# Pairs of pooled attention on Trainium2: values multiplied ahead of later scores, and chunks 3 to 5 made known twelve steps sooner

## The chip, the cores and the metric

The kernel runs on one core of one Trainium2 chip. The metric is device time of one execution in microseconds; a lower one is better. The other cores of the chip are idle.

## The reference

An attention is followed by two feed-forward networks, all in fp32:

```
q, k, v: 4 batches, 8 heads, 576 positions, 64 wide
pooled:  q, k, v averaged over groups of 4 positions (144 of them), softmax(q k^T / 8) v, each row repeated 4 times
local:   softmax of q k^T / 8 where |i - j| < 4, times v
x = pooled + local, as 2304 rows of 512
h = x @ w_in (512 x 2048);   x2 = (h * cos h) @ w_out (2048 x 512)
out = (((x2 @ w1) * (x2 @ w2)) @ w3) @ w_out2    (w1, w2: 512 x 1024, w3: 1024 x 1024)
```

## The kernel before, in words

The program is one long order of instructions, which a small planner in the kernel writes at build time: it holds a list of jobs (Python generators), each with an urgency (a lower number goes first), and a guess of how long every operation takes (`cost`, `LATENCY`). Whenever an engine is free in that guess, it is given the first job in the order of urgency whose inputs are ready by the guess. On the chip each engine then follows its own list in order, with semaphores between the engines. All operations go through one helper, so that nearly every instruction carries its line, L137 (L138 in the changed kernel); groups are told apart by their tiles.

The stages, in the order in which TensorE (PE) comes to them:

- **Weights w3 and w_out2** are multiplied into one matrix (`w5_job`, tile `ps_w`), with the attention of the first chunks between them. PE fills what is left with products of zeros (`ps_z`, `ps_w<-zeros`).
- **First network.** The rows are cut into 6 chunks of 384. A step is a chunk and one of the 16 slices of the inner width, 96 steps in all: `h_job` makes `ps_h` (12 products), `chain_job` turns it into g = h cos h on ScalarE (ACT), VectorE (DVE) and GpSimd (POOL), and `y_job` adds g times w_out to four banks (12 products, `ps_y`). The h of a step may be up to four steps ahead of its y (`LAG`). Chunk 0 takes 12 of its steps (`HALF`), then chunk 1 comes in.
- **Second network** (`ps_ab`, `ps_o`), from step 96 on.

The attention runs beside it. Its local part is done in units of 192 positions, two to a chunk (`unit_job`; scores `ps_sb`, softmax in `sc`, transposes `ps_tb`, values `ps_av`, then the sum with the pooled part in `xs`). Its pooled part is done in pairs of heads, four to a batch (`pair_job`; scores `ps_s`, softmax in `sd`, transposes `ps_t`, copies `ptp` of these, products with values `ps_t<-ptp` or `ps_p<-ptp`, result `up`). A unit needs all four pairs of its batch before its values, and h of a chunk needs both of its units. Batches 0 and 1 take the softmax of a pair's scores straight from PSUM with a bias; batches 2 and 3 through `sd` and GpSimd.

In `pair_job` the products of pair p - 1 with its values go right behind the transposes of pair p, in columns 288 to 431 of the first of the two banks that these fill, and ACT then reads `up` from there. Four PSUM banks (`bank`) are shared by h and the attention; while h runs, the attention may hold two of them (`banks`). A pair's `ptp` and `vd` have one buffer each, `sd` two. ACT holds one table of functions at a time, and exp of the attention and sin of the chain are in different ones, so each visit of exp during the first network costs two table loads; `exps` gathers waiting ones.

The loop at the end of `fused_kernel` tells the planner of a chunk's attention when h has reached a step: of chunk 2 early, and of chunk i from 3 on when the first step of chunk i - 1 is done (`first[i - 1] + 1`, which is 33, 49 and 65).

Of the kernel before, what the change touches and what calls it, by code (L numbers as in the profile page):

```python
# [14 lines left out]
AF = mybir.ActivationFunctionType  # L15
# [5 lines left out]
B, H, S, D = 4, 8, 576, 64  # L21
# [7 lines left out]
KC = DM // P  # L29
SD = S // 4  # L30
# [16 lines left out]
HALF = 12  # L47
# [8 lines left out]
EARLY_WARM, RISEN, REST = 3000.0, 10000.0, 130.0  # L56
FIRST, SLACK = 3000.0, 1150.0
TOGETHER, PATIENCE = 4, 6750.0
A0, A1 = 6.0, 6

U_QK, U_PAIR, U_POOL, U_UNIT = -12, -14, -10.5, -9.0
# [14 lines left out]
def fused_kernel(ctx: ExitStack, tc: tile.TileContext, qk_block, v_block, qk_pool, v_pool,  # L76
# [96 lines left out]
    def buf(slot, name, shape, dtype=F32):  # L173

        pool, size, _ = slots[slot[0]]
        item = 8 if dtype == I64 else 4
        t = pool.tile([P, size // item], dtype, name=name, tag=f"{slot[0]}{slot[1]}", bufs=1)
        t = t[:, :math.prod(shape)]
        if len(shape) == 1:
            return t  # L180
        names = "abcd"[:len(shape)]
        return t.rearrange(f"p ({' '.join(names)}) -> p {' '.join(names)}", **dict(zip(names, shape)))
# [6 lines left out]
    def bank(n, name):  # L189

        return psum.tile([P, 512], F32, name=name, tag=f"bank{n}", bufs=1)
# [18 lines left out]
    def on(name, fn, *aps, when=lambda: True):  # L210
        yield name, fn, aps, when

    def until(cond):
        while not cond():
            yield "until", cond
# [4 lines left out]
    def take(name, n=1, spare=lambda: 0):  # L220

        yield from until(lambda: len(at_hand(name)) >= n + spare())
        got = at_hand(name)[:n]
        for x in got:
            free[name].remove(x)
        return got[0][1] if n == 1 else [x[1] for x in got]
# [15 lines left out]
    def give(name, slot, engine):  # L242
        free[name].append((ends[engine] + LATENCY[engine], slot))
# [5 lines left out]
    def count(key, n=1):  # L249
        done[key] = done.get(key, 0) + n  # L250

    def reached(key, n):
        return lambda: done.get(key, 0) >= n


    def banks(n):
        yield from until(lambda: done.get("banks", 0) + n <= (2 if done.get("h", 0) else 4))
        count("banks", n)
        got = []
        for _ in range(n):  # L260
            got.append((yield from take("bank")))
        return got
# [146 lines left out]
    up_t = {}  # L409
# [42 lines left out]
    with_values = {}  # L452

    def pair_job(b, p):
        early, bias = b < EARLY, b < BIAS
        yield from until(reached("sd", b * KC + p))
        fs = yield from take("sd")
        count("sd")
        f = buf(fs, "sd", [2, 2, SD])[:QP]
        sums, nms = small(fs, "sums", [2, 2], QP), small(fs, "nm", [2, 2], QP)  # L460
        if early:
            yield from until(reached(("pooled", b), UPB))
            qk = pool_qk[b][0][:, p]
        else:
            qs = yield from take("qkd")
            raw_slot = yield from take("raw")
            raw = buf(raw_slot, "qkr", [2, SD, 4])
            yield from on("sy", lambda: sy.dma_start(out=raw, in_=qk_pool[b, p]))
            qk = buf(qs, "qkd", [2, SD])
            for side in range(2):  # L470
                yield from on("ve", lambda: ve.tensor_reduce(out=qk[:, side], in_=raw[:, side], axis=AX.X, op=ALU.add), raw)
            give("raw", raw_slot, "ve")
        ns = yield from banks(2)
        ps = [bank(n, "ps_s") for n in ns]

        def scores():

            for c in range(2):
                for r in range(2):
                    rs = slice(r * D, (r + 1) * D)  # L480
                    pe.matmul(ps[r][:QP, c * SD:(c + 1) * SD], lhsT=qk[rs, 0, c * QP:(c + 1) * QP], rhs=qk[rs, 1, :], start=True, stop=True)

        yield from on("pe", scores, qk)
        if not early:
            give("qkd", qs, "pe")
        elif p == KC - 1:
            give("raw", pool_qk[b][1], "pe")
        for r in range(2):
            s, nm = ps[r][:QP, :2 * SD].rearrange("p (c k) -> p c k", c=2), nms[:, r]
            yield from on("ve", lambda: ve.tensor_reduce(out=nm, in_=s, axis=AX.X, op=ALU.max, negate=True), ps[r])  # L490
            if bias:
                continue
            yield from on("ve", lambda: ve.tensor_tensor(out=f[:, r], in0=s, in1=nm.unsqueeze(2).to_broadcast([QP, 2, SD]), op=ALU.add), nms)
            give_bank(ns[r], "ve")
        if bias:
            yield from on("ve", lambda: ve.tensor_scalar_mul(nms, nms, SCALE / 16.0), nms)

            def exp():
                for r in range(2):
                    for c in range(2):  # L500
                        se.activation(out=f[:, r, c], in_=ps[r][:QP, c * SD:(c + 1) * SD], func=AF.Exp, scale=SCALE / 16.0,
                                      bias=nms[:, r, c:c + 1], accum_out=sums[:, r, c:c + 1])
                    give_bank(ns[r], "se")

            yield from exps(exp, nms)
        else:
            yield from exps(lambda: se.activation(out=f, in_=f, func=AF.Exp, scale=SCALE / 16.0), f)
            yield from on("ve", lambda: ve.tensor_reduce(out=sums, in_=f, axis=AX.X, op=ALU.add), f)

        def div():  # L510
            ve.tensor_scalar_add(sums, sums, 1e-9)
            ve.reciprocal(sums, sums)

        yield from on("ve", div, sums)
        each, by = ("ve", ve) if b < BY_VE else ("ge", ge)
        yield from on(each, lambda: by.tensor_tensor(out=f, in0=f, in1=sums.unsqueeze(3).to_broadcast([QP, 2, 2, SD]), op=ALU.mult), sums)

        yield from until(lambda: not p or (b, p - 1) in with_values)
        before = with_values.pop((b, p - 1)) if p else None
        ns = yield from banks(2)  # L520
        psts = [bank(n, "ps_t") for n in ns]

        def turn():
            for r in range(2):
                for kc in range(2):
                    for c in range(2):
                        o = (kc * 2 + c) * QP
                        pe.transpose(psts[r][:QP, o:o + QP], f[:, r, c, kc * QP:(kc + 1) * QP], ident[:QP, :QP])

        def values(of, pso):  # L530
            v, t = of[:2]
            for kc in range(2):
                for r in range(2):
                    pe.matmul(pso[r * D:(r + 1) * D], lhsT=v[:, kc, r * D:(r + 1) * D], rhs=t[:, r, kc * SD:(kc + 1) * SD], start=kc == 0, stop=kc == 1)
            give("vd", of[2], "pe")
            give("ptp", of[3], "pe")

        if b not in up_t:
            slot = yield from take("up")
            up_t[b] = buf(slot, "up", [KC, SD]), slot  # L540
        up = up_t[b][0]
        if p:
            pso = psts[0][:, 2 * SD:3 * SD]
            yield from on("pe", lambda: (turn(), values(before, pso)), f, *before[:2])
        else:
            yield from on("pe", turn, f)
        give("sd", fs, "pe")
        tsl = yield from take("ptp")
        t = buf(tsl, "ptp", [2, 2 * SD])[:QP]
        for r in (1, 0):  # L550
            yield from on("se", lambda: se.copy(t[:, r], psts[r][:QP, :2 * SD]), psts[r])
            if r == 0 and p:
                yield from on("se", lambda: se.activation(out=up[:, p - 1, :], in_=pso, func=AF.Copy, scale=0.25), psts[0])
                count(("pairs", b))
            give_bank(ns[r], "se")
        yield from until(lambda: (b, p) in pool_vs)
        v, vs = pool_vs.pop((b, p))
        if p < KC - 1:
            with_values[b, p] = v, t, vs, tsl
            return  # L560
        n = (yield from banks(1))[0]
        pso = bank(n, "ps_p")
        yield from on("pe", lambda: values((v, t, vs, tsl), pso[:, :SD]), v, t)
        yield from on("se", lambda: se.activation(out=up[:, p, :], in_=pso[:, :SD], func=AF.Copy, scale=0.25), pso)
        give_bank(n, "se")
        count(("pairs", b))
# [484 lines left out]
    with tc.manual_schedule():  # L1051
# [60 lines left out]
        Job(W5 + 1000.5, y_job())  # L1112
        attention(1, W5 + first[1] - A1)
        for i in range(2, NC1):
            run(reached("h", first[i - 1] + 1 if i > 2 else first[0] + HALF + 1))
            attention(i, W5 + first[i])
            if i == 2:
                for f in range(F2):
                    Job(W5 + first[2] + 4 * f, w12_job(f))
# [68 lines left out]
```

## Time and profile before

| | |
|---|---|
| median of 3 runs | 845.57 us (843.66 to 848.01) |
| span of the profiled execution, first to last instruction (the profile has no other time of it) | 843.8 us |
| PE busy | 827.2 us (98%) |
| DVE, ACT, POOL busy | 515.3, 444.1, 371.5 us |
| mean granted clock of TensorE | 0.996 |
| chain of waits, share of PE | 87% |

Times in the rows are counted from the first instruction. A busy PE is one with a matrix product under way; "idle before" is the time in which an engine had nothing under way, and the arrow names what ended it. The granted clock is 1.00 at 2.4 GHz and 0.50 at 1.2 GHz. A matrix product in fp32 (scores, values, transposes, `ps_w`) shows as two records.

### The profile page before, as it was taken

To read this page: it belongs to the slowest core of one execution; us is meant where nothing else is said; L and a number is where in the kernel's file an instruction comes from. 1 tells how busy PE (TensorE), PEld (TensorE's weight loads), DVE (VectorE), ACT (ScalarE), POOL (GpSimd) and SP (SyncE) were. 2 spreads that over 40 slices of the span, in tenths; PEclk is the share of its full clock that TensorE was granted. 3 is DMA by queue.
4 is the path that set the end of the run, shared out by engine and by line. 5 is a ranking of instruction groups with operands and counts; after the bars stand their busy time and mean duration, and the time that the engine had idled before them with its cause. 6 is when DMAs were issued, how large, how long until landed. Compare 5 with 4: busy or idle time off the path is not lost.

```text
span 843.8 us, 15678 instructions
## 1 busy us (share of the span) xinstructions
PE 827.2 (98%) x5982; PEld 752.2 (89%) x5982; DVE 515.3 (61%) x924; ACT 444.1 (53%) x900; POOL 371.5 (44%) x330
## 2 busy tenths in 40 slices
PE   7999999999999999999989999999999999999998
PEld 7544599999999999999989999999999899999997
DVE  5987889995547785778566434734435544463442
ACT  2746698877767676867658565632113211231112
POOL 0112559865443355434635434524335632363322
PEclk9999999999999999999999999999999999999999
DMA  9998896131445553545452328692001400020002
GB/s 268 289 309 288 290 343 240 41 113 50 150 143 169 151 161 118 169 144 158 139 165 73 101 100 301 246 402 99 26 13 53 149 26 26 24 90 26 26 26 75
DMA packets 61402, 121.87 MB, mean 144 GB/s; under 512 B 18960, under 2 KB 26384, under 8 KB 61328
## 3 DMA queue, kind: packets, MB, share of 16 engines
q1 hardware_dynamic: 54432, 112.12, 41.4%
q10 hardware_dynamic: 6896, 8.76, 3.0%
q8 instruction: 47, 0.77, 0.4%
q14 instruction: 27, 0.22, 0.1%
HBM read 93.07 MB, written 27.79 MB: 143 GB/s over the span
## 4 chain that ended last, share of the span: by engine, by line
PE 87%; DVE 5%; ACT 3%; DMA 2%; issue 1%; POOL 1%; ACTq 0%; SPq 0%; DVEq 0%; POOLq 0%
PE ps_y L137 21%; PE ps_ab L137 20%; PE ps_h L137 20%; PE ps_o L137 12%; PE ps_w L137 7%; DVE t L137 3%; PE ps_t L137 2%; PE ps_av L137 1%; PE ps_tb L137 1%; PE ps_s L137 1%; PE ps_sb L137 1%; DVE c L137 1%; DMA vr<-v_pool 1%; POOL wo L137 1%; ACT c L137 1%
## 5 line engine op out<-in xcount | busy, mean ns | idle before, releaser
L137 PE MATMUL ps_h<-xs,wi 128*128 128x384 f32 x1152 | 221.7, 339 | 3.3 <-DVE c L137 2.2
L137 PE MATMUL ps_y<-g,wo 128*128 128x384 f32 x1152 | 220.9, 337 | 0.5 <-POOL g L137 0.5
L137 PEld LDWEIGHTS ps_h<-xs,wi 128*128 128x128 f32 x1152 | 201.3, 189 | 7.2 <-DVE c L137 2.5
L137 PEld LDWEIGHTS ps_y<-g,wo 128*128 128x128 f32 x1152 | 199.8, 188 | 2.9 <-issue 1.5
L137 PE MATMUL ps_ab<-y,w 128*128 128x384 f32 x1008 | 184.9, 336 | 0.9 <-DVE v L137 0.8
L137 PEld LDWEIGHTS ps_ab<-y,w 128*128 128x128 f32 x1008 | 176.7, 188 | 6.6 <-issue 1.4
L137 DVE TENSOR_TENSOR v<-v,ps_ab 128x384 f32<-128x384 f32 x168 | 90.8, 553 | 134.9 <-ACT w L137 74.0
L137 POOL TENSOR_TENSOR g<-c,g 128x384 fp32r<-128x384 f32 x96 | 107.3, 1118 | 145.4 <-ACT g L137 125.8
L137 ACT ACTIVATE c<-c 128x384 f32<-128x384 f32 x192 | 100.5, 524 | 34.4 <-DVE c L137 31.6
L137 POOL TENSOR_TENSOR v<-v 128x384 f32<-128x384 f32 x48 | 49.7, 1038 | 145.2 <-DVE v L137 143.4
L137 PE MATMUL ps_o<-w,m 128*128 128x512 f32 x432 | 107.3, 392 | 0.0
L137 ACT CAST m<-v 128x384 fp32r<-128x384 f32 x48 | 24.5, 514 | 142.9 <-POOL v L137 142.9
L137 PEld LDWEIGHTS ps_o<-w,m 128*128 128x128 f32 x432 | 80.3, 188 | 14.1
L137 DVE SCALAR_TENSOR_TENSOR c<-turns,ps_h 128x384 f32<-128x384 int32 x96 | 52.7, 549 | 63.0 <-ACT turns L137 61.1
L137 DVE SCALAR_TENSOR_TENSOR c<-c,ps_h 128x384 f32<-128x384 f32 x96 | 52.7, 549 | 46.5 <-ACT c L137 46.2
L137 ACT CAST g<-c 128x384 fp32r<-128x384 f32 x96 | 49.2, 512 | 37.1 <-DVE c L137 35.0
L137 ACT ACTIVATE turns<-ps_h 128x384 int32<-128x384 f32 x96 | 46.8, 487 | 36.7 <-PE ps_h L137 36.0
L137 PE MATMUL ps_w<-w,w 128*128 128x512 f32 x128 | 59.5, 604 | 1.0 <-DVE w L137 1.0
L137 ACT ACTIVATE t<-raw 128x512 f32<-128x512 f32 x72 | 47.8, 677 | 15.9 <-DMA raw<-w3t 3.4
L137 DVE TENSOR_SCALAR t<-t 128x512 int32<-128x512 int32 x72 | 51.0, 723 | 7.6 <-ACT t L137 7.6
L137 POOL TENSOR_TENSOR m<-v,m 128x384 fp32r<-128x384 f32 x48 | 47.8, 1016 | 0.0
L137 POOL TENSOR_TENSOR sc<-sc,bmax 128x1024 f32<-128x1024 f32 x12 | 24.3, 2026 | 49.4 <-DVE bmax L137 39.7
(89 smaller groups left out, 856.7 us busy)
## 6 DMA issues: line engine op xcount, KB each, us to landing
w_sc<-w SPq DMA_DIRECT2D x56, 256.0 KB
w<-w_sc SPq DMA_DIRECT2D x28, 512.0 KB
raw<-w SPq DMA_DIRECT2D x24, 512.0 KB
raw<-w3t SPq DMA_DIRECT2D x16, 512.0 KB
raw<-w_in SPq DMA_DIRECT2D x16, 512.0 KB
raw<-w_out SPq DMA_DIRECT2D x16, 512.0 KB
qkr<-qk_pool SPq DMA_DIRECT2D x12, 576.0 KB
vb<-v_block SPq DMA_DIRECT2D x48, 128.0 KB
```

The lines of the kernel that those rows point to most:

```text
L137: return call(*args, **kw)
```

## The change

In `pair_job` the products of a pair with its values move: those of pair p - 2 now go in front of the scores of pair p (p = 2, 3), in the same columns of the first scores' bank, in one piece with these scores, and ACT reads `up` from there ahead of DVE's maxima. Only pair 2's products still go behind pair 3's transposes, and pair 3's own come last, as before. So pair p's scores now ask that pair p - 2's copies are made, and the transposes of pairs 1 and 2 ask that the scores of the pair behind are done. And the planner hears of the attention of chunks 3, 4 and 5 when h has reached 21, 37 and 53 instead of 33, 49 and 65. Numbers of instructions stay the same, but for one product of zeros less on PE (11 in `ps_w` instead of 12) and two more table loads on ACT (24 instead of 22).

```
--- before.py
+++ after.py
@@ -56,6 +56,7 @@
 EARLY_WARM, RISEN, REST = 3000.0, 10000.0, 130.0
 FIRST, SLACK = 3000.0, 1150.0
 TOGETHER, PATIENCE = 4, 6750.0
+AHEAD = 12
 A0, A1 = 6.0, 6
 
 U_QK, U_PAIR, U_POOL, U_UNIT = -12, -14, -10.5, -9.0
@@ -470,8 +471,22 @@
             for side in range(2):
                 yield from on("ve", lambda: ve.tensor_reduce(out=qk[:, side], in_=raw[:, side], axis=AX.X, op=ALU.add), raw)
             give("raw", raw_slot, "ve")
+        yield from until(lambda: p < 2 or (b, p - 2) in with_values)
+        before = with_values.pop((b, p - 2)) if p >= 2 else None
         ns = yield from banks(2)
         ps = [bank(n, "ps_s") for n in ns]
+        if b not in up_t:
+            slot = yield from take("up")
+            up_t[b] = buf(slot, "up", [KC, SD]), slot
+        up = up_t[b][0]
+
+        def values(of, pso):
+            v, t = of[:2]
+            for kc in range(2):
+                for r in range(2):
+                    pe.matmul(pso[r * D:(r + 1) * D], lhsT=v[:, kc, r * D:(r + 1) * D], rhs=t[:, r, kc * SD:(kc + 1) * SD], start=kc == 0, stop=kc == 1)
+            give("vd", of[2], "pe")
+            give("ptp", of[3], "pe")
 
         def scores():
 
@@ -480,7 +495,14 @@
                     rs = slice(r * D, (r + 1) * D)
                     pe.matmul(ps[r][:QP, c * SD:(c + 1) * SD], lhsT=qk[rs, 0, c * QP:(c + 1) * QP], rhs=qk[rs, 1, :], start=True, stop=True)
 
-        yield from on("pe", scores, qk)
+        if before:
+            pso = ps[0][:, 2 * SD:3 * SD]
+            yield from on("pe", lambda: (values(before, pso), scores()), qk, *before[:2])
+            yield from on("se", lambda: se.activation(out=up[:, p - 2, :], in_=pso, func=AF.Copy, scale=0.25), ps[0])
+            count(("pairs", b))
+        else:
+            yield from on("pe", scores, qk)
+        count(("scores", b))
         if not early:
             give("qkd", qs, "pe")
         elif p == KC - 1:
@@ -515,8 +537,9 @@
         each, by = ("ve", ve) if b < BY_VE else ("ge", ge)
         yield from on(each, lambda: by.tensor_tensor(out=f, in0=f, in1=sums.unsqueeze(3).to_broadcast([QP, 2, 2, SD]), op=ALU.mult), sums)
 
-        yield from until(lambda: not p or (b, p - 1) in with_values)
-        before = with_values.pop((b, p - 1)) if p else None
+        last = p == KC - 1
+        yield from until((lambda: (b, p - 1) in with_values) if last else reached(("scores", b), p + 2) if p else lambda: True)
+        before = with_values.pop((b, p - 1)) if last else None
         ns = yield from banks(2)
         psts = [bank(n, "ps_t") for n in ns]
 
@@ -527,19 +550,7 @@
                         o = (kc * 2 + c) * QP
                         pe.transpose(psts[r][:QP, o:o + QP], f[:, r, c, kc * QP:(kc + 1) * QP], ident[:QP, :QP])
 
-        def values(of, pso):
-            v, t = of[:2]
-            for kc in range(2):
-                for r in range(2):
-                    pe.matmul(pso[r * D:(r + 1) * D], lhsT=v[:, kc, r * D:(r + 1) * D], rhs=t[:, r, kc * SD:(kc + 1) * SD], start=kc == 0, stop=kc == 1)
-            give("vd", of[2], "pe")
-            give("ptp", of[3], "pe")
-
-        if b not in up_t:
-            slot = yield from take("up")
-            up_t[b] = buf(slot, "up", [KC, SD]), slot
-        up = up_t[b][0]
-        if p:
+        if last:
             pso = psts[0][:, 2 * SD:3 * SD]
             yield from on("pe", lambda: (turn(), values(before, pso)), f, *before[:2])
         else:
@@ -549,13 +560,13 @@
         t = buf(tsl, "ptp", [2, 2 * SD])[:QP]
         for r in (1, 0):
             yield from on("se", lambda: se.copy(t[:, r], psts[r][:QP, :2 * SD]), psts[r])
-            if r == 0 and p:
+            if r == 0 and last:
                 yield from on("se", lambda: se.activation(out=up[:, p - 1, :], in_=pso, func=AF.Copy, scale=0.25), psts[0])
                 count(("pairs", b))
             give_bank(ns[r], "se")
         yield from until(lambda: (b, p) in pool_vs)
         v, vs = pool_vs.pop((b, p))
-        if p < KC - 1:
+        if not last:
             with_values[b, p] = v, t, vs, tsl
             return
         n = (yield from banks(1))[0]
@@ -1112,7 +1123,7 @@
         Job(W5 + 1000.5, y_job())
         attention(1, W5 + first[1] - A1)
         for i in range(2, NC1):
-            run(reached("h", first[i - 1] + 1 if i > 2 else first[0] + HALF + 1))
+            run(reached("h", first[i - 1] + 1 - AHEAD if i > 2 else first[0] + HALF + 1))
             attention(i, W5 + first[i])
             if i == 2:
                 for f in range(F2):
```

The planner answers with another order on every engine. Three places matter for the prediction.

**PE, the first steps of the first network** (`ps_sb` and `ps_tb` are of local units, `ps_s` and `ps_t` of batch 1's pairs). Before:

```order
L137 MATMUL ps_sb<-kb,qb 64x64 x32
L137 MATMUL ps_w_919<-w_750,w_973 128x512
L137 MATMUL ps_h<-xs,wi 128x384 x48
L137 MATMUL ps_t<-ident,sd 72x72 x8
L137 MATMUL ps_t<-ptp,vd 64x144 x4
L137 MATMUL ps_y_1403<-g,wo 128x384 x3
L137 MATMUL ps_y_1434<-g,wo 128x384 x3
```

And in the changed kernel:

```order
L138 MATMUL ps_sb<-kb,qb 64x64 x32
L138 MATMUL ps_w_895<-w_777,w_996 128x512
L138 MATMUL ps_w_903<-w_777,w_996 128x512
L138 MATMUL ps_w_923<-w_777,w_996 128x512
L138 MATMUL ps_h<-xs,wi 128x384 x48
L138 MATMUL ps_y_1374<-g,wo 128x384 x3
L138 MATMUL ps_s<-ptp,vd 64x144 x4
L138 MATMUL ps_s<-qkd 72x144 x4
L138 MATMUL ps_y_1389<-g,wo 128x384 x3
```

The transposes and values that stood between the first four steps of h and the first y are gone from there; the pair's next piece (values and scores) comes only behind the first three products of y.

**POOL, around its first g** (`wi`, `wo`: weights of the first network; `sc`: a unit's softmax; `g`: the low half of a step's g). Before:

```order
L137 TENSOR_TENSOR xs<-xb,xs 128x2x4x48
L137 TENSOR_TENSOR wo<-t,wo 128x512
L137 TENSOR_TENSOR g<-c,g 128x384 x3
L137 TENSOR_TENSOR sc<-sc,bmax 128x1024
L137 TENSOR_TENSOR wi<-t,wi 128x512
```

In the changed kernel:

```order
L138 TENSOR_TENSOR xs<-xb,xs 128x2x4x48 x2
L138 TENSOR_TENSOR wo<-t,wo 128x512
L138 TENSOR_TENSOR sc<-sc,bmax 128x1024
L138 TENSOR_TENSOR g<-c,g 128x384
L138 TENSOR_TENSOR wi<-t,wi 128x512
L138 TENSOR_TENSOR g<-c,g 128x384
```

The unit's `sc` has moved from behind the third g to in front of the first.

**PE, h step 64, the first of chunk 4.** Before, from the values of chunk 4's second unit on (`ps_y` has four banks, each with its number):

```order
L137 MATMUL ps_y_4296<-g,wo 128x384 x3
L137 MATMUL ps_av<-pt,vb 64x48 x32
L137 MATMUL ps_y_4303<-g,wo 128x384 x3
...
L137 MATMUL ps_y_4296<-g,wo 128x384 x3
L137 MATMUL ps_y_4303<-g,wo 128x384 x3
L137 MATMUL ps_h<-xs,wi 128x384 x33
L137 MATMUL ps_sb<-kb,qb 64x64 x32
```

The nine rows of y behind these values are 27 products. In the changed kernel, at the same step (the `ps_av` here is of chunk 5's first unit; chunk 4's two stand in front of h steps 49 and 57):

```order
L138 MATMUL ps_h<-xs,wi 128x384 x12
L138 MATMUL ps_y_4561<-g,wo 128x384 x3
L138 MATMUL ps_av<-pt,vb 64x48 x32
L138 MATMUL ps_y_4589<-g,wo 128x384 x3
L138 MATMUL ps_y_4597<-g,wo 128x384 x3
L138 MATMUL ps_y_4602<-g,wo 128x384 x3
L138 MATMUL ps_h<-xs,wi 128x384 x12
```

Where h ran out of x and y was used up before, a step of h and a step of y now alternate without a break.

## Rows read from the trace of the kernel before

**Rows 1.** The page: span, busy time of each engine, PE's granted clock in 40 slices.

```profile
span 843.8 us, 15678 instructions
PE 827.2 (98%) x5982; PEld 752.2 (89%) x5982; DVE 515.3 (61%) x924; ACT 444.1 (53%) x900; POOL 371.5 (44%) x330
PEclk9999999999999999999999999999999999999999
```

**Rows 2.** Waits of PE: who waited for whom, us in total, times, longest.

```profile
PE ps_h L137 <- DVE c L137: 2.2, 1, 2.2
...
PE ps_sb L137 <- DVE sc L137: 1.3, 1, 1.3
PE ps_s L137 <- DVE sc L137: 1.2, 1, 1.2
...
PE ps_h L137 <- POOL wi L137: 1.1, 2, 0.8
...
PE ps_tb L137 <- POOL sc L137: 0.4, 1, 0.4
```

**Rows 3.** Timeline of PE around h step 64: start, us, operation, records, idle before.

```profile
413.23 4.95 PE L137 MATMUL ps_y<-g,wo 128*128 128x384 f32 x27
418.03 4.33 PE L137 MATMUL ps_h<-xs,wi 128*128 128x384 f32 x24
424.55 3.25 PE L137 MATMUL ps_h<-xs,wi 128*128 128x384 f32 x9 [2.20 <-DVE c L137]
...
435.11 1.16 PE L137 MATMUL ps_sb<-kb,qb 64*64 64x64 f32 x64 [0.25 <-issue]
```

**Rows 4.** Windows there: length, busy by engine (records), granted clock, DMA, GB/s.

```profile
422.00:424.00 2.00, 0.35 (x2) 0.03 (x1) 0.06 (x1) 1.57 (x4) 0.00 (x0) 1.00 0.96 356
424.00:426.00 2.00, 1.45 (x5) 1.45 (x6) 0.96 (x2) 1.73 (x4) 0.88 (x1) 0.61 0.03 12
426.00:428.00 2.00, 2.00 (x18) 1.56 (x21) 0.56 (x1) 0.58 (x2) 0.84 (x2) 0.53 0.00 0
428.00:430.00 2.00, 2.00 (x70) 1.93 (x63) 1.01 (x2) 0.31 (x1) 0.28 (x1) 1.00 0.04 8
```

**Rows 5.** Timeline of PE, first steps of the first network.

```profile
102.87 8.89 PE L137 MATMUL ps_h<-xs,wi 128*128 128x384 f32 x48
111.61 0.41 PE L137 MATMUL ps_t<-ident,sd 72*72 72x72 f32 x4
112.24 0.44 PE L137 MATMUL ps_t<-ident,sd 72*72 72x72 f32 x4 [0.22 <-DVE c L137]
112.61 0.71 PE L137 MATMUL ps_t<-ptp,vd 72*64 72x144 f32 x8
113.78 2.35 PE L137 MATMUL ps_y<-g,wo 128*128 128x384 f32 x12 [0.46 <-POOL g L137]
```

**Rows 6.** Timeline of POOL in the same stretch.

```profile
110.42 1.90 POOL L137 TENSOR_TENSOR wo<-t,wo 128x512 fp32r<-128x512 f32 x1 [4.72 <-ACT wo L137]
112.27 2.42 POOL L137 TENSOR_TENSOR g<-c,g 128x384 fp32r<-128x384 f32 x2
...
120.70 1.90 POOL L137 TENSOR_TENSOR sc<-sc,bmax 128x1024 f32<-128x1024 f32 x1 [0.80 <-DMA raw<-w_in]
```

**Rows 7.** Timeline of ACT in the same stretch.

```profile
107.22 1.28 ACT L137 ACT_TABLE_LOAD   x1
108.52 0.53 ACT L137 ACTIVATE c<-c 128x384 f32<-128x384 f32 x1
...
117.35 1.07 ACT L137 ACTIVATE sc<-sc 128x1024 f32<-128x1024 f32 x1
```

**Rows 8.** Timeline of DVE in the same stretch.

```profile
109.95 0.54 DVE L137 SCALAR_TENSOR_TENSOR c<-c,ps_h 128x384 f32<-128x384 f32 x1
...
118.45 1.22 DVE L137 TENSOR_REDUCE bmax<-sc 128x16 f32<-128x1024 f32 x1 [0.16 <-ACT sc L137]
```

**Rows 9.** Timeline of PE at the longest wait of steps 12 to 20.

```profile
171.62 1.62 PE L137 MATMUL ps_sb<-kb,qb 64*64 64x64 f32 x64 [1.32 <-DVE sc L137]
```

**Rows 10.** Window behind that wait, columns as in rows 4.

```profile
172.00:174.00 2.00, 1.92 (x67) 1.85 (x68) 2.00 (x5) 1.66 (x4) 2.00 (x2) 1.00 0.27 98
```

**Rows 11.** Groups of ACT: busy us, mean ns, idle before.

```profile
L137 ACT ACTIVATE up<-ps_t 128x144 f32<-128x144 f32 x12 | 3.6, 299 | 0.0
```

## Prediction

> **What bounds the kernel now.** I read the page first: of the 843.8 us of the span PE has a product under way in 827.2, and its clock is granted in full in nearly every slice [rows 1]. The products stay the same, so the change can win only what PE loses: the 16.6 us in which it is idle, and any stretch at half clock. The waits of PE then say where these lie [rows 2]. The longest one is 2.2 us, before h, released by a c on DVE; waits of 1.3, 1.1 (two of them) and 0.4 us lie in the first twenty steps. The others stand ahead of the first network or in the second one, where the change alters little.
>
> The timeline shows what the longest wait is [rows 3]. Nine rows of y run in one piece, 27 products: h of step 64 lacks its x, because chunk 4's attention is late, and y eats up the four steps that h was ahead. Then h makes two steps, nothing is left for y, and PE stands for 2.20 us, until the chain of ACT, DVE and POOL has freed a bank. The windows show a second price [rows 4]: from 424 to 428 the granted clock is 0.61 and 0.53, so the 1.2 GHz level after that idle time, and 1.00 again from 428. At 171.62 PE was idle for 1.32 us [rows 9] and the clock stayed at 1.00 [rows 10].
>
> The second stretch to read is the start of the first network [rows 5]. Four steps of h run from 102.87 to 111.61; the first y starts at 113.78. Of these 2.17 us only 0.22 + 0.46 = 0.68 are idle: a pair's transposes and values fill the other 1.49.
>
> **A, the stall at step 64.** In the new order the units of chunk 4 are done eight and more steps ahead, and h and y alternate there. The 2.20 us go, the 0.25 of the scores behind it [rows 3], and the half clock: (1 - 0.61) x 2 + (1 - 0.53) x 2 = 1.72 us [rows 4]. A = -4.2. The ends are -4.2 and 0 (another chunk starves instead). The attention's own products only change their place.
>
> **B, the first y.** The filler of 1.49 us is gone from its gap; its work comes later and takes its time there. With g as early as before, PE idles the whole 2.17 instead of 0.68. Is g as early? Before, the first g on POOL starts at 112.27, behind a wo of 1.90 [rows 6]. Now the unit's sc, also 1.90, stands between that wo and g; and this sc needs an exp of 1.07 on ACT, which now runs ahead of the table load [rows 7], and a sum of 1.22 on DVE, which now runs ahead of the first c that leaves the chain at 109.95 [rows 8]. Before, both came after it (117.35 and 118.45). The wo is done earlier in exchange. So g comes between 0 and 1.9 us later; I take 0.5, since one GpSimd piece of 1.90 stands directly ahead of g in either order. That is a gap of 2.7 with nothing in it, 2.0 more than the 0.68. Such a gap is longer than the 2.20 that was followed by the low clock and twice the 1.32 that was not, so I add 1.72. B = +3.7. Its ends are 0 (the gap closes by another order of arrival) and 2.17 + 1.90 - 0.68 + 1.72 = +5.1.
>
> The Trainium skill, "TensorE: Matmul & The Clock Gate", Part 1, says that the gate has just these two levels, and that the same kernel shows a different number of slow products from one run to the next. By that the 1.72 of A and of B may each be absent from a run; A + B would lie between -2.2 (slow stretch in A alone) and +1.2 (in B alone), against -0.5 in my sum. The rows agree on the two levels; one profile cannot show the scatter.
>
> **C, the other waits of steps 1 to 20.** The two waits for wi (1.1 us together [rows 2]) come from a POOL that works without a break; its sc of 1.90 at 120.70 [rows 6] is now done before them. I let them go: C = -1.1. The waits of 1.32 and 0.4 I leave as they are. Ends: all 2.8 go, or as much comes on top.
>
> **What I cost at nothing.** Two more table loads, 1.28 each [rows 7]: ACT is busy for 53% [rows 1], and h is up to four steps ahead of y. Where that lead is used up, a visit of exp is on the path, with its loads. One product of zeros less: under 0.2. The moved products ahead of the first network: PE is full there, and what is done later frees as much time now; a new wait in this in-order list could cost 0 to 1.2, as its nearest row (`ps_s` for DVE [rows 2]). The DMAs: the last load of a pair's q and k of batch 1 and the loads of chunks 3 to 5 move on SP; those of 3 to 5 come sooner, and no wait of PE names a load. The weights of the second network are ready about two steps later, still ahead of step 96.
>
> A wait is added: ACT's read of `up` and DVE's maxima of the scores now share a bank, so the maxima follow a read of 0.30 us [rows 11] eight times, and the chain's pieces on DVE stand behind them. The lead of h hides it; in the open it would be 2.4 us at least. The Trainium skill, "PSUM — Partial Sum Buffer", on bank collisions, says that two engines may not use one bank and quadrant at once, reads included; that is why this is a wait and not an overlap. No row here shows its price.
>
> **Sum.** -4.2 + 3.7 - 1.1 = -1.6 us: a span of 842.2. The span of before lies 1.8 below the median of the runs, 845.57, so the time is 845.57 - 1.6 = **844.0 us**. A measurement of this kernel can tell about 0.5% from no change, 4.2 us; the forecast is no change.
>
> **Rivals.**
>
> *The gap at the first y does not open* (faster): the chain comes sooner, or the order of arrival puts the pair's scores into it. For it: h starts some 2 us sooner, while DVE and ACT have their conversions of weights behind them earlier. Against it: the banks for these scores are freed only by the c of the chain. Then -4.2 - 1.1 = -5.3: 840.3 us. With the gap as it is but no slow clock, -3.3: 842.3, still no change.
>
> *The early attention takes the lead of h away* (slower). One mechanism: visits of exp put loads of 2 x 1.28 and the exp of 1.07 between a step's two pieces on ACT, now spread over chunks 2 to 4, with the new wait on DVE in the same steps. It decides when a chain is late by more than the lead of h, some three steps of about 4.2 us (a step of h and one of y). Each such place costs what step 64 cost, 2.20 + 1.72 = 3.9. With two of them: -1.6 + 7.8 = +6.2, 851.8 us. Against it: before, ten such visits passed without a wait of PE.
>
> *The stall only moves* (no change): x of chunk 2, whose second unit now ends two steps ahead of its use, is late in place of chunk 4. Then A = 0, and the sum is +2.6: 848.2.
>
> **How the numbers follow.** Forecast 0.45, gap closed 0.30, lead lost 0.15, stall moved 0.10. The forecast case reaches below -4.2 in a few parts of a hundred, when more of C goes. So faster by over 0.5% 0.32, within 0.5% 0.53, slower 0.15. The range takes in A, and all of C with B at 0, -7.0, at the low end (838.5), and at the high end the moved stall with a late g (850); it leaves out the rival of lost lead.
>
> **What would show it.** Right: no run of more than about 12 products of y without h at step 64, and a clock of 1.00 there; PE idle for 2 to 3.5 us between the first four steps of h and the first y, released by g of POOL, with a clock near 0.5 for some 3.5 us behind it; waits for wi under 0.5. Wrong: a full PE at the first y (then the first rival), or new waits of h or y for a c or a g between steps 20 and 66 (then the second), or at step 32 (then the third).

## The result, and the profile after

The changed kernel takes 852.35 us (median of 6 runs, 850.61 to 855.41) against 846.22 for the kernel before (6 runs beside it): 6.1 us more, a ratio of 1.0080 with a 95% interval of 1.0063 to 1.0097. It is slower, by more than the 0.5% that can be told from no change, and lies above the range of the prediction (838.5 to 850).

The page of the changed kernel (span, busy time, granted clock in 40 slices), for [rows 1]:

```profile
span 853.5 us, 15677 instructions
PE 832.0 (97%) x5981; PEld 754.6 (88%) x5981; DVE 521.9 (61%) x924; ACT 446.7 (52%) x902; POOL 374.5 (44%) x330
...
PEclk9899979999999999999999999999999999999999
```

PE is idle for 21.5 us instead of 16.6, and two slices show a lower clock. The one in the second lies ahead of the first network, and it does not come from the order of instructions: e9 below has the same order and a 9 there. This profile is of the longest of the six runs (mean clock 0.988, the others 0.992 to 0.994), and the runs of the kernel before alone have mean clocks of 0.993 to 1.000. The 7 in the sixth slice is the place to read. The view of waits, for [rows 2]:

```profile
PE ps_y L138 <- POOL g L138: 5.1, 1, 5.1
...
PE ps_h L138 <- DVE c L138: 1.2, 1, 1.2
```

The 2.2 us of h for a c, step 64, are gone. In their place stands one wait of 5.1 us: the first y. The timeline of PE there, for [rows 5]:

```profile
104.91 8.89 PE L138 MATMUL ps_h<-xs,wi 128*128 128x384 f32 x48
118.93 1.33 PE L138 MATMUL ps_y<-g,wo 128*128 128x384 f32 x3 [5.12 <-POOL g L138]
120.18 1.23 PE L138 MATMUL ps_s<-ptp,vd 72*64 72x144 f32 x8
121.34 1.24 PE L138 MATMUL ps_s<-qkd 64*72 64x144 f32 x8
122.51 4.21 PE L138 MATMUL ps_y<-g,wo 128*128 128x384 f32 x12
126.52 2.42 PE L138 MATMUL ps_h<-xs,wi 128*128 128x384 f32 x12
```

From the first h to the fifth step of h it took 21.61 us. In the kernel before it was 13.10, from 102.87 [rows 5] to the start of the fifth step:

```profile
115.97 2.24 PE L137 MATMUL ps_h<-xs,wi 128*128 128x384 f32 x12
```

That stretch of before has three products of y less, which are 0.52 at the 2.08 us that twelve take from start to start. So the stretch lost 8.0 us. Windows, columns as in [rows 4]:

```profile
116.00:118.00 2.00, 0.00 (x0) 0.00 (x0) 2.00 (x4) 2.00 (x6) 1.95 (x2) 0.65 0.79 184
...
124.00:126.00 2.00, 2.00 (x8) 2.00 (x7) 2.00 (x5) 1.97 (x5) 1.72 (x2) 0.50 1.03 412
126.00:128.00 2.00, 2.00 (x11) 2.00 (x10) 2.00 (x4) 0.75 (x2) 0.72 (x1) 0.79 1.03 414
420.00:430.00 10.00, 10.00 (x116) 9.70 (x115) 5.42 (x10) 7.73 (x13) 4.17 (x4) 1.00 0.37 120
```

The clock falls while PE stands and stays at its lower level until 126 to 128; around step 64 (last row) it is 1.00 and PE is never idle. There h and y alternate, for [rows 3]:

```profile
426.33 0.69 PE L138 MATMUL ps_y<-g,wo 128*128 128x384 f32 x3
426.94 1.15 PE L138 MATMUL ps_av<-pt,vb 64*64 64x48 f32 x64
428.02 1.83 PE L138 MATMUL ps_y<-g,wo 128*128 128x384 f32 x9
429.69 2.24 PE L138 MATMUL ps_h<-xs,wi 128*128 128x384 f32 x12
```

Why g is late, ACT tells (timeline, for [rows 7]; `DMA_DIRECT2D` is a store of `w5_out_job`, the profile writes its tile without the number):

```profile
104.41 0.33 ACTq L132 DMA_DIRECT2D w_sc<-w  x1
...
107.59 0.49 ACT L138 ACTIVATE turns<-ps_h 128x384 int32<-128x384 f32 x1
111.84 0.66 ACT L138 ACTIVATE t<-raw 128x512 f32<-128x512 f32 x1 [3.75 <-DMA w_sc<-w]
112.40 1.05 ACT L138 ACTIVATE sc<-sc 128x1024 f32<-128x1024 f32 x1
113.46 1.28 ACT L138 ACT_TABLE_LOAD   x1
114.76 0.52 ACT L138 ACTIVATE c<-c 128x384 f32<-128x384 f32 x1
...
116.94 0.50 ACT L138 CAST g<-c 128x384 fp32r<-128x384 f32 x1
```

A conversion of a weight (`t<-raw`) stands ahead of the unit's exp and of the first sin. It waits 3.75 us for a store. In the kernel before a conversion stands in the same place, ahead of the table load, and it waits for nothing:

```profile
106.55 0.66 ACT L137 ACTIVATE t<-raw 128x512 f32<-128x512 f32 x1
```

POOL of the changed kernel, for [rows 6]:

```profile
107.66 1.36 POOL L138 TENSOR_TENSOR wo<-t,wo 128x512 fp32r<-128x512 f32 x1 [1.77 <-ACT wo L138]
115.57 1.90 POOL L138 TENSOR_TENSOR sc<-sc,bmax 128x1024 f32<-128x1024 f32 x1 [6.55 <-DVE bmax L138]
117.52 1.35 POOL L138 TENSOR_TENSOR g<-c,g 128x384 fp32r<-128x384 f32 x1
```

POOL is done with wo early and stands for 6.55 us until exp and sum have come through. g starts 12.61 us behind h's start; before it was 9.40.

### The profile page after: what moved, and what is told of

It is laid out like the page before. It is cut to its first block, busy times and chain, and to the rows that moved or that the text cites. A ratio compares the mean times of both kernels' runs of the same rounds, so it can differ in the third digit from the quotient of the medians.

```text
span 853.5 us, 15677 instructions
## 1 busy us (share of the span) xinstructions
PE 832.0 (97%) x5981; PEld 754.6 (88%) x5981; DVE 521.9 (61%) x924; ACT 446.7 (52%) x902; POOL 374.5 (44%) x330
## 4 chain that ended last, share of the span: by engine, by line
PE 83%; DVE 8%; DMA 4%; issue 2%; ACT 2%; POOL 1%; SPq 0%; ACTq 0%; DVEq 0%; POOLq 0%
PE ps_ab L138 20%; PE ps_y L138 20%; PE ps_h L138 19%; PE ps_o L138 12%; PE ps_w L138 7%; DVE t L138 4%; PE ps_s L138 2%; PE ps_av L138 1%; DVE c L138 1%; PE ps_t L138 1%; PE ps_sb L138 1%; DVE bmax L138 1%; DMA w_sc<-w 1%; PE ps_tb L138 1%; DMA vr<-v_pool 1%
## 5 line engine op out<-in xcount | busy, mean ns | idle before, releaser
L138 PE MATMUL ps_y<-g,wo 128*128 128x384 f32 x1152 | 223.9, 340 | 5.1 <-POOL g L138 5.1
L138 PE MATMUL ps_w<-w,w 128*128 128x512 f32 x128 | 62.4, 630 | 1.0 <-DVE w L138 1.0
L138 DVE TENSOR_SCALAR t<-t 128x512 int32<-128x512 int32 x72 | 55.4, 783 | 8.9 <-ACT t L138 8.6
L138 PEld LDWEIGHTS ps_w<-w,w 128*128 128x128 f32 x128 | 23.9, 198 | 26.4 <-issue 23.0
```

The source lines that it names most:

```text
L138: return call(*args, **kw)
```

## The experiments

All are compared with the kernel before, run beside them on the same chip. The stretch is that from the first h to the fifth step of h, less 0.52 for three more products of y where they lie in it; its loss is against 13.10. In e8 the idle time does not stand at the first y but ahead of it, around the fourth step of h.

| run | median us | ratio, 95% | idle at first y | loss of stretch |
|---|---|---|---|---|
| the change | 852.35 | 1.0063 to 1.0097 | 5.12 | 8.0 |
| e1, no notice | 878.07 | 1.0365 to 1.0408 | 5.33 | 7.6 |
| e2, notice only | 845.49 | 0.9979 to 1.0007 | 0.47 | 0.0 |
| e3, late pairs | 841.95 | 0.9945 to 0.9968 | 0.47 | 0.0 |
| e4, g slots | 847.96 | 1.0019 to 1.0045 | 5.93 | 8.8 |
| e5, no store wait | 845.05 | 0.9980 to 1.0000 | 0.89 | 1.0 |
| e6, filled gap | 848.83 | 1.0019 to 1.0046 | filled | 5.5, with 5.4 of filler |
| e7, batch 1 as before | 843.80 | 0.9961 to 0.9987 | 1.59 | 2.1 |
| e8, batch 0 as before | 848.12 | 1.0007 to 1.0034 | 2.34 + 2.09 | 6.3 |
| e9, same order | 848.81 | 1.0028 to 1.0055 | 3.25 | 5.6 |
| e10, late pairs, no notice | 856.98 | 1.0111 to 1.0155 | 0.47 | 0.0 |
| e11, notice of 16 | 845.01 | 0.9982 to 1.0009 | 0.47 | 0.0 |

### The parts of the change

By the notice is meant the number of steps by which the planner hears of a chunk's attention sooner (`AHEAD`). e1 is the changed kernel with `AHEAD = 0`, e2 the kernel before with `- AHEAD` in the loop, e3 the change with

```
-        yield from until(lambda: p < 2 or (b, p - 2) in with_values)
-        before = with_values.pop((b, p - 2)) if p >= 2 else None
+        moved = b >= 2
+        yield from until(lambda: not moved or p < 2 or (b, p - 2) in with_values)
+        before = with_values.pop((b, p - 2)) if moved and p >= 2 else None
...
+        behind = last or not moved and p > 0
```

and `behind` in place of `last` where the transposes are made. The first 20 steps are ordered as in the changed kernel in e1, and as in the kernel before in e2 and e3.

> The changed kernel with the planner told of chunks 3 to 5 as late as before; the first 20 steps are in the changed kernel's order, and the plan lets y use up h's whole lead at two steps, 48 and 64. Theory (the loss lies at the first y, the gain at step 64): the loss stays and the gain goes, with a second stall at step 48: +4 to +8 against the changed kernel, 856 to 860 us, 10 to 14 above before; PE idle over 3 us at the first y and over 1.5 us at step 64. Rival (the early notice takes the lead of h away and makes the loss): below the changed kernel, 845 to 849, with no idle time over 1 us between steps 20 and 66 that the changed kernel lacks.

> The kernel before with the earlier notice alone; its order is that of before up to some step 29. Theory: the gain of step 64 without the loss at the first y: 4 us less than before, 841 to 843; no idle time over 1 us at step 64, 0.7 us at the first y. Rival (early notice is what costs): 848 to 852, with new waits of h or y between steps 20 and 66.

> The whole change, but the values move only in batches 2 and 3; the order is that of before up to some step 29. Theory: as the notice alone, 841 to 843, within 1.5 us of it, since the moved values of later batches have h's lead above them. Rival (the moved values cost in every batch, by the new wait of DVE on ACT): 4 or more above the notice alone, 846 to 850.

e1 is 25.7 us above the change where I expected 4 to 8, and not in the way of the rival: the idle time of the first y stayed, and two long stalls came, at steps 48 and 64. Waits of its timeline around step 64:

```profile
445.39 1.97 PE L138 MATMUL ps_tb<-ident,sc 128*128 128x128 f32 x8 [9.27 <-POOL sc L138]
452.54 7.20 PE L138 MATMUL ps_h<-xs,wi 128*128 128x384 f32 x24 [3.29 <-POOL xs L138]
```

e2 lost nothing at the first y and has no stall at step 64 (clock 1.00 and PE full from 400 to 430), as the theory had it; but its time is that of before, not 4 us less. e3 is what the theory gave, 4.2 us below before by the medians (0.43% by the ratio, interval 0.32 to 0.55%), and the fastest of all kernels here. Its windows around step 64:

```profile
416.00:426.00 10.00, 10.00 (x118) 9.66 (x119) 4.61 (x12) 6.96 (x16) 6.72 (x8) 1.00 0.52 161
426.00:436.00 10.00, 10.00 (x59) 10.00 (x58) 5.90 (x10) 7.30 (x16) 2.33 (x3) 1.00 0.46 158
```

So the loss lies with the values moved in the early batches, 0 and 1; with the earlier notice the stall at step 64 is gone, in e2 as in e3. Why e2 stays behind e3 I did not settle. Two new waits are part of it, from its timeline:

```profile
243.22 0.63 PE L138 MATMUL ps_tb<-ident,sc 128*128 128x128 f32 x4 [0.87 <-DVE sums L138]
...
316.94 0.82 PE L138 MATMUL ps_t<-ident,sd 72*72 72x72 f32 x8 [0.39 <-DVE sc L138]
```

e3 has only 0.24 us of such waits from step 20 to step 72. The same kind of scatter showed in two more runs of e3's code, with `AHEAD` at 0 (e10) and at 16 (e11):

> The values move in batches 2 and 3 only, and the planner is told of chunks 3 to 5 as late as before; y uses up h's lead at steps 48 and 64 in the plan. Theory (the move lengthens a batch's chain, so that without the notice chunks 3 and 4 come late): stalls of several us at steps 48 and 64 as in the run with the changed kernel's order and no notice, and nothing lost at the first y: 865 to 872. Rival (those stalls came from the early batches' new order): 843 to 850.

> The values move in batches 2 and 3 only, with a notice of sixteen steps in place of twelve. Theory (twelve steps already take the whole stall away, and what is left of idle time lies elsewhere): within 1.5 us of the twelve steps' 841.95. Rival (a longer notice takes away more): 840 or less.

e10 kept the stall at step 64 and lost 11 us, less than I expected: at step 48 only 0.57 us of idle time came. Without the notice the late move costs; with it, it wins. e11 fits neither theory: 3 us slower than twelve steps, with waits of PE of 0.96 and 0.59 us at 210 and 255 that e3 has not. Twelve is a good value here, and not the start of a trend.

### Which batch empties the gap

e7 is the change with `moved = b != 1`, e8 with `moved = b >= 1`.

> The whole change, but batch 1's values stay behind its transposes, so the gap before the first y has its filler again. Theory (the loss comes from batch 1's moved values alone): idle under 1.5 us at the first y, no low clock behind it, 841 to 844. Rival (batch 0's moved values, ahead of the first network, cost by themselves): 845 or more.

> The whole change, but batch 0's values stay behind its transposes. The values and scores of a pair of batch 1 stand between the third and the fourth step of h, and nothing stands between the fourth and the first y. Theory (batch 1's move empties the gap): idle over 2 us at the first y and a low clock behind it, 848 to 853. Rival (batch 0's move makes g late): g as early as in the kernel before, 842 to 845.

e7 came out by the theory in time, but not in its idle time: 1.59 us ahead of the second half of the transposes, and the low clock behind it, for 3.4 us. Its line and windows:

```profile
113.75 0.44 PE L138 MATMUL ps_t<-ident,sd 72*72 72x72 f32 x4 [1.59 <-DVE c L138]
...
114.00:116.00 2.00, 2.00 (x15) 1.57 (x13) 2.00 (x4) 2.00 (x6) 1.01 (x2) 0.64 1.03 404
116.00:118.00 2.00, 2.00 (x8) 2.00 (x8) 1.68 (x3) 1.98 (x6) 2.00 (x2) 0.51 1.06 274
```

e8 has the time of its theory, but not the place: at the first y PE does not stand. It stands twice ahead of it, for banks that a c on DVE frees, and the last step of h ahead of y runs at half clock:

```profile
112.17 0.71 PE L138 MATMUL ps_s<-qkd 64*72 64x144 f32 x6 [2.34 <-DVE c L138]
114.97 4.21 PE L138 MATMUL ps_h<-xs,wi 128*128 128x384 f32 x12 [2.09 <-DVE c L138]
```

In e8 ACT's conversion waits for a store as well:

```profile
108.23 0.67 ACT L138 ACTIVATE t<-raw 128x512 f32<-128x512 f32 x1 [2.96 <-DMA w_sc<-w]
```

Without batch 1's move the stretch loses 2.1 us instead of 8.0, so this move opens most of the gap. It is not alone. By the ratios, batch 0's move costs 0.17% by itself (e7 against e3), but 0.60% on top of batch 1's (the change against e8). What the two do together beyond their sum these runs do not separate, since each brings another plan.

### The store ahead of g

e4 sends stores 0, 2 and 4 of w5 out of buffers of g, which are free until the first network:

```
-        slot = yield from take("t")
+        slot = yield from take("g" if f in (0, 2, 4) else "t")
...
-        give_stored("t", slot, w5_sc[f])
+        give_stored(slot[0], slot, w5_sc[f])
```

> The changed kernel, but three of the eight stores of w5 go out from buffers of g, which are empty until the first network, so that fewer buffers of t wait for a store. Theory (the conversion on ACT that stands ahead of the unit's exp and of the first sin waited 3.75 us for such a store, and this alone made g late): that wait falls under 1 us, g comes 3 us or more sooner, PE idles 1 to 2.5 us at the first y, and the time is 846 to 849. Rival (the wait is for the load of the weight itself or for a crowded DMA): the wait stays at 3 us or more, and the time within 2 us of the changed kernel's.

The wait stayed, 4.87 us on ACT (5.93 at y): I had moved the wrong stores. The conversion's buffer was that of store 5. The run does not speak for the rival, then; it is 4.4 us faster than the changed kernel for reasons elsewhere that I did not follow; its plan differs from that of the change from the first y on, and its POOL makes the first g ahead of sc. e5 takes the buffer by `take({5: "st", 6: "g", 7: "g"}.get(f, "t"))`.

> The changed kernel, but the last three stores of w5 go out from other buffers (one of st, two of g), so that no conversion on ACT ahead of the first g takes a buffer that such a store still reads; the order of PE is that of the changed kernel up to the first y. (In the run with g's buffers for stores 0, 2 and 4 the conversion took the buffer of store 5, which I had left in t, and waited 4.87 us.) Theory (this wait made g late): no wait of ACT over 1 us between the first turns and the first g, PE idle for 1 to 2.5 us at the first y, 845 to 848 us. Rival (the unit's exp, sum and product ahead of g are what makes it late): idle time over 4 us, 850 or more.

e5 did what the theory said and a little more (0.89 us idle), but it proves less than it seems: in its plan the first g also goes ahead of the unit's sum on DVE and ahead of sc on POOL. So e9 changes nothing in the order of any engine: the traces of the changed kernel and of e9 have the same instructions in the same order on each. It only sends the three stores out of other memory and keeps the planner's accounts:

```
-        w = buf(slot, "w5", [512])
+        w = buf({5: ("st", 0), 6: ("g", 1), 7: ("g", 2)}.get(f, slot), "w5", [512])
```

The conversion in the instruction lists, in the changed kernel and in e9 (the names are counters that a DMA raises when it has landed; DMAHW5 is raised by its own load, DMAHW0 by store 5):

```
L138 ACTIVATE t_1302<-raw_1237 128x512 [waits DMAHW5_49,DMAHW0_49]
L138 ACTIVATE t<-raw 128x512 [waits DMAHW5_49]
```

> The changed kernel in exactly its own order on all engines; only the memory that the last three stores of w5 go out from is other (st, and two of g), so that the conversion ahead of the unit's exp waits for no store. Theory (this one wait made g late, and the low clock followed): the conversion waits under 0.5 us, sin starts some 6.5 us behind h's start instead of 9.9, PE idles 1 to 2.5 us at the first y, and the time is 845 to 848. Rival (the order itself, with the unit's exp and product ahead of g, costs most of it): idle time of 3.5 us or more, and 849.5 or more.

ACT of e9, from its timeline:

```profile
103.19 0.49 ACT L138 ACTIVATE turns<-ps_h 128x384 int32<-128x384 f32 x1 [0.17 <-PE ps_h L138]
103.57 0.66 ACT L138 ACTIVATE t<-raw 128x512 f32<-128x512 f32 x1
104.14 1.05 ACT L138 ACTIVATE sc<-sc 128x1024 f32<-128x1024 f32 x1
105.20 1.28 ACT L138 ACT_TABLE_LOAD   x1
106.72 0.53 ACT L138 ACTIVATE c<-c 128x384 f32<-128x384 f32 x1 [0.23 <-DVE c L138]
```

PE of e9:

```profile
100.50 8.90 PE L138 MATMUL ps_h<-xs,wi 128*128 128x384 f32 x48
112.65 0.84 PE L138 MATMUL ps_y<-g,wo 128*128 128x384 f32 x3 [3.25 <-POOL g L138]
...
115.74 4.21 PE L138 MATMUL ps_y<-g,wo 128*128 128x384 f32 x12
119.75 2.41 PE L138 MATMUL ps_h<-xs,wi 128*128 128x384 f32 x12
```

The wait is gone, sin starts 6.2 us behind h's start instead of 9.9, and the kernel is 0.39% nearer to before, some 3.3 us. But the idle time is 3.25 and the time lies between the two theories: the store is one part, the order the other. POOL's sc still stands ahead of g there (109.29 to 111.15, when g starts), and DVE's sum ahead of the c.

### Idle time or its clock

e6 is the changed kernel with, behind the fourth step of h,

```
+            if n == LAG:
+                yield from take("bank7")
+                spare = bank(7, "ps_z")[:, :N1]
+                yield from on("pe", lambda: [pe.matmul(spare, lhsT=w[:, 0, :P], rhs=xh[:, 0, :], start=True, stop=True) for _ in range(30)])
+                give("bank7", 0, "pe")
```

> The changed kernel with 30 more products (128 by 384, some 4.8 us by those of h) behind the fourth step of h, into a bank that nobody reads, and the moved values and scores behind them, ahead of the first y: the gap is filled and g is as late as before. Theory (the low clock behind the first y follows from the idle time): clock 1.00 in the 12 us behind the first y, idle time there under 1.5 us, and 3 to 4 us less than the changed kernel: 848 to 850. Rival (the clock falls there for another reason, or the products only add their own time): 852 to 857.

PE of e6, from its timeline:

```profile
109.62 5.37 PE L138 MATMUL ps_z<-xs,wi 128*128 128x384 f32 x30
...
117.25 2.36 PE L138 MATMUL ps_y<-g,wo 128*128 128x384 f32 x12
119.46 2.35 PE L138 MATMUL ps_h<-xs,wi 128*128 128x384 f32 x12
```

ACT's wait for the store is 4.69 us in this run, so g is no earlier; yet 30 idle products more make the kernel 0.47% faster than the change, by the ratios. The windows from 110 to 126 all show 1.00, and twelve products of y take 2.36 where they took 4.21. What is saved is the clock: filler and the idle time that is left (5.3 and 0.60 us) take more time than the 5.12 of idle time did, and the stretch still loses 2.5 us less. The rest of the gain, some 1.5 us, I did not follow; this plan, too, is another one behind the first y.

## Why the prediction was wrong

**A, right at its place.** No long run of y at step 64, clock 1.00 there, PE full. The 4.2 us of before are gone, but 1.7 came back between steps 20 and 66 (0.88 at 213.56, 0.58 at 403.21, 0.23 at 436.42), where the kernel before has no wait but that stall. The moved values alone do not make them: e3 moves them in the batches of these steps as well, and has 0.24. That the rest of the order makes them is likely, but no run shows it by itself.

**B, the step that failed.** I took +3.7 with an upper end of +5.1; the stretch lost 8.0. By its parts: idle time 5.12 instead of 0.68, +4.4; and the low clock, against the same products at 1.00: three of y 1.33 for 0.79, the values and scores 2.47 for 1.42 (both as in e5), twelve of y 4.21 for 2.24, h 2.42 for 2.24, so +3.7. Both were mis-sized.

- *Is g as early?* I let POOL's sc, ACT's exp and DVE's sum decide that and bounded it by one piece of 1.90. e9 shows this part alone: g 10.65 behind h's start instead of 9.40, 1.25 later, inside my 0 to 1.9 though I took 0.5; idle time +2.6 for a forecast of +2.0. What I left out is the list of ACT ahead of the exp. The conversion there takes a buffer that a store still reads. This is another 1.9 us of idle time (5.12 - 3.25). It is not the only reason that 5.1 was no upper end: e9, without it, still loses 5.6, because of the clock.
- *The low clock.* I gave the gap the 1.72 of step 64 [rows 4]. The slow stretch there ended at 428, 3.5 us behind the idle time; here it ended at 126.8, 7.9 us behind it, and in e9 at 120.5, 7.8 us behind a shorter gap. So the price was about twice the one that I took, 3.7 for 1.72. That it hangs on the idle time e6 shows: with the gap filled the clock stays at 1.00.

The Trainium skill, "TensorE: Matmul & The Clock Gate", Part 1, was cited for two levels and for a count of slow products that differs between runs. The rows agree on the levels, and the mean clocks of the kernel before's runs (0.993 to 1.000) on the scatter. I drew only a lower price from that scatter, none that could also be higher; the row gives the higher one.

**C, wrong and small.** The waits of steps 4 to 20 were to lose 1.1 us; they are 0.25, 1.03, 1.16 and 0.21, so 2.65 where before had 2.82. A wait for wi of 1.03 is still among them; the earlier sc did not take it away.

**What I cost at nothing.** The DMAs were the mistake. "No wait of PE names a load" is true, and says nothing about a wait of ACT for a store. The table loads cost nothing that can be seen: e3 has four more of them than before (26 for 22), and is the fastest. The new wait of DVE on ACT was there, 2.08 us at 122.94 in the changed kernel, and nothing of PE waited for it there. The new wait in PE's own list, which I had put at 0 to 1.2 and left out of the sum, was there as well, at the first moved values of batch 0:

```profile
41.61 0.71 PE L138 MATMUL ps_s<-ptp,vd 72*64 72x144 f32 x8 [0.56 <-DVE vd L138]
```

e7 and e9 wait for the same 0.56 at this place; e3 and e8, which leave batch 0 as it was, have no such wait.

**The sum.** +8.0 - 4.2 + 1.7 - 0.2 = +5.3, at the lower end of the ratio's interval (+5.3 to +8.2 us) and 0.8 under the medians' 6.1. With the 0.56 of batch 0 it is +5.9; the last 0.2 lie within the spread of the runs. The profiled run is longer still (9.7 us): eight records of `ps_w` at 25.04, ahead of the first network, take 6.77 us there and 3.70 in the kernel before; the clock is 0.72 from 20 to 30.

**The rivals.** None held. The lead of h was not used up; the stall did not move; the gap did not close. The loss was the forecast's own term B, at over twice its size.

## What to carry to other kernels

When a change empties the time ahead of a first dependence, walk back along the list of every engine up to the releaser, and ask of each instruction in it not only whose result it reads but whose buffer it writes, and who still reads that: a store counts. An order written by a planner moves everything at once, so test a suspected wait by changing memory alone and keeping the order (e9), and a suspected gap by filling it (e6). Keep the part of a change that wins: here the move in the last two batches with the notice (e3) takes 841.95 us, 0.43% under the kernel before and 1.2% under the changed one.

## What the runs showed of the hardware

The store that the conversion waited for, 256 KB, was issued at 104.41 and waited for until 111.84, 7.4 us; the median of the eight is 3.9. The DMA views of the changed kernel tell where the time went (queue, packets, MB, share of 16 engines; q10, by its bytes over the whole run, is the one of ACT's stores, q1 that of SP's loads). From 105 to 108, where q10 has no packet:

```profile
q1 hardware_dynamic: 308, 0.90, 96.0%
```

From 109 to 112:

```profile
q1 hardware_dynamic: 221, 0.82, 67.8%
q10 hardware_dynamic: 215, 0.41, 35.2%
```

So more than half of the 7.4 us passed before a packet of the store moved: none is there from 105 to 108, and 14 in the microsecond behind it. Up to then SP's loads had the engines, 1.9 MB of which SP had issued between 102.77 and 104.10, ahead of the store. Why the store's packets come only then no row shows. The Trainium skill, "DMA: Bandwidth & Descriptors", section "Queues, rings and completion order", says that an engine takes turns between its queues, a packet at a time. The rows agree once both queues have packets: 221 and 215 in 109 to 112. The loads' packets are the larger ones, so that they get two thirds of the bytes.

The price of idle time is not one figure per gap. 1.32 us of it left the clock at 1.00 [rows 9, 10]; 1.59 in e7 was followed by the low clock for 3.4 us and 2.20 at step 64 by 3.5; behind 3.25 in e9 the low clock fell on 7.2 us of work, behind 5.12 in the changed kernel on 7.9, and behind 5.33 in e1 on 6.2. A longer gap does not always cost more.
